# Transposing q and k by DMA instead of on TensorE, in an attention kernel with a gated feed-forward behind it

## The chip, the cores and the metric

The kernel runs on one core of a Trainium2 chip. The metric is the device time of one execution in microseconds (us). The kernel before took 457.21 us, the median of three runs (457.0 to 460.33).

## The reference

There are 8 batches of 8 heads, 576 query positions and a head width of 64. Sixteen "beacon" keys and values stand ahead of the 576 others in every head, so a query sees 592 keys: all beacons, and the keys up to its own position.

```python
k_all = np.concatenate([beacon_k, k], axis=2)          # (8, 8, 592, 64)
v_all = np.concatenate([beacon_v, v], axis=2)
scores = scale * np.matmul(q, k_all.transpose(0, 1, 3, 2))
scores = np.where(causal, -1e9, scores)
a = np.exp(scores - scores.max(-1, keepdims=True))
a /= a.sum(-1, keepdims=True) + 1e-09
x = np.matmul(a, v_all)                                # heads side by side: 4608 tokens x 512
g = x @ w_gate                                         # 512 x 1536
out = (g / (1 + np.exp(-g)) * (x @ w_val)) @ w_out     # 1536 x 512
```

Inputs and the output are fp32. The kernel casts to bf16 and multiplies in bf16.

## The kernel before, in words

**Layout.** q, k and v of one batch are loaded with the position on the partitions: five pieces (`c` = 0 to 4) of up to 128 positions by 8 heads by 64, in fp32 staging tiles `q32`, `k32`, `v32`. VectorE casts q and k to the bf16 tiles `qb` and `kb`, piece by piece; GpSimd casts v to one of two tiles `vb`. The score matmul (line 176) contracts over the head width, so it needs q and k with the head width on the partitions. That is the task of the two transposing functions: for a pair `m` of heads (2 x 64 = 128 columns) they run five TensorE transposes of 128x128 into a PSUM tile `t_ps`, and then one copy brings the whole pair to SBUF, as `qT[m]` or `kT[m]` (128 partitions x 640). There is one PSUM buffer for `t_ps`, the attention outputs `pv_ps` and the transposed `xt_ps` together (pool `att`, one buffer).

**Stages of a batch.** The order of the work is written out by hand, and each engine takes its instructions in that order.

- Attention: for each of the four pairs, `scores1` and `scores2` (matmuls into PSUM, Exp on ScalarE, causal masks on GpSimd), the product with v (`pv`), and `x_transpose`, which writes the result into `xT`. In the gaps stand eight halves of the last feed-forward matmul of the chunk before (`fill`, lines 267 to 278), each second one with a copy to SBUF and a store.
- Feed-forward of 512 tokens: 12 steps `f`, each eight matmuls of 128x512 for the gate and the value (line 244), Silu on ScalarE (254) and a product on VectorE (255). Of the first three steps, three quarters of the matmuls are issued between the last parts of the attention. The big PSUM pool has three buffers, which scores and gate/value products share.
- Preparing the next batch, inside the feed-forward: from step `f_cast` on two casts are issued in each step (lines 364 to 369). When all ten are out, and from step 4 on, one transposing function follows in each step (370); what is left comes behind step 11 (372). k pairs are copied from PSUM by VectorE, q pairs by ScalarE. `f_cast` is 0, but 7 in the first batch, whose data for the next batch are still loading.
- Then SyncE gets the loads of the batch after next (374). They wait until the casts have freed the staging tiles.

The first batch is prepared pair by pair by `prep_first`, in which every step waits for the loads. A last feed-forward of 512 tokens follows the eighth batch. SyncE issues all loads of q, k and v and all stores, in the order of the program; the weights are loaded from GpSimd's queue.

Of the kernel before, what the change touches and what calls it, by code (L numbers as in the profile page):

```python
# [8 lines left out]
ACT = mybir.ActivationFunctionType  # L9
ALU = mybir.AluOpType  # L10
BF16 = mybir.dt.bfloat16
FP32 = mybir.dt.float32

P = 128
# [3 lines left out]
NKT = 5  # L18
KPAD = NKT * P
# [24 lines left out]
def kernel(  # L44
# [12 lines left out]
    nc = tc.nc  # L57
    B, H, Sq, Dq = q.shape
# [7 lines left out]
    NPAIR = H // 2  # L66
    assert NCH == B + 1

    static = ctx.enter_context(tc.tile_pool(name="static", bufs=1))
# [13 lines left out]
    qb = static.tile([P, NKT, H, D], BF16, name="qb")  # L83
    kb = static.tile([P, NKT, H, D], BF16, name="kb")
    vb = [static.tile([P, NKT, H, 68], BF16, name=f"vb{i}") for i in range(2)]
    qT = [static.tile([P, KPAD], BF16, name=f"qT{m}") for m in range(NPAIR)]
    kT = [static.tile([P, KPAD], BF16, name=f"kT{m}") for m in range(NPAIR)]
    pt = [
        (static.tile([P, P1_W], BF16, name=f"p1_{i}"), static.tile([P, P2_W], BF16, name=f"p2_{i}"))
        for i in range(4)  # L90
# [29 lines left out]
    def load_batch(b):  # L120
        load_kv("k32", k, beacon_k, b, 0, H)
        load_q(b, 0, H)
        load_kv("v32", v, beacon_v, b, 0, H)

    def cast_pieces(dst, name, h0, h1, last, engine):
        src = stage[name]

        def main(c0, c1):
            engine.tensor_copy(dst[:, c0:c1, h0:h1, 0:D], src[:, c0:c1, h0:h1, :])  # L129

        def tail():
            engine.tensor_copy(dst[0:last, 4, h0:h1, 0:D], src[0:last, 4, h0:h1, :])

        if h1 - h0 == H:
            return [lambda c=c: main(c, c + 1) for c in range(4)] + [tail]
        return [lambda: main(0, 4), tail]

    def load_w(i):
        cols = slice(384 * i, 384 * i + 384)
        for t, src in ((wg, moe_w_gate), (wv, moe_w_val)):  # L140
            nc.gpsimd.dma_start(t[:, :, cols], src[:, cols].rearrange("(kk p) f -> p kk f", p=P))
# [8 lines left out]
    def transpose_q(m, copy):  # L150
        t_ps = att.tile([P, KPAD], BF16, name="t_ps", tag="att")
        for c in range(NKT):
            nc.tensor.transpose(t_ps[:, P * c : P * c + P], qb[:, c, 2 * m : 2 * m + 2, :], ident[:])  # L153
        copy(qT[m][:, 0:S], t_ps[:, 0:S])

    def transpose_k(m, copy):
        t_ps = att.tile([P, KPAD], BF16, name="t_ps", tag="att")
        for c in range(NKT):
            L = P if c < 4 else 80
            nc.tensor.transpose(  # L160
                t_ps[:, P * c : P * c + L], kb[0:L, c, 2 * m : 2 * m + 2, :], ident[0:L, 0:L]
            )
        copy(kT[m][:, 0 : NB + S], t_ps[:, 0 : NB + S])

    def dve_copy(o, i):
        nc.vector.tensor_copy(o, i)  # L166

    def act_copy(o, i):
        nc.scalar.activation(o, i, ACT.Copy)  # L169

    def scores(m, which, spec, used, masks):
        s = [big.tile([P, 1024], FP32, name="s_ps", tag="big") for _ in range(2)]
# [24 lines left out]
    def scores1(m):  # L197
        scores(m, 0, SCORES1, P1_USED, MASKS1)

    def scores2(m):  # L200
        scores(m, 1, SCORES2, P2_USED, MASKS2)

    def pv(b, m, hh, x):
        h = 2 * m + hh
        o_ps = att.tile([P, NKT, 68], FP32, name="pv_ps", tag="att")
        for c, (q0, _) in enumerate(QBLOCKS):
            for t in range(c + 1):
                w, col = p_slice(t, q0)
                nc.tensor.matmul(  # L209
                    o_ps[:, c, 0 : D + 1],  # L210
                    lhsT=pt[2 * (m % 2) + hh][w][:, col : col + P],
                    rhs=vb[b % 2][:, t, h, 0 : D + 1],
                    start=(t == 0),
                    stop=(t == c),
                )
        rec = rec_pool.tile([P, NKT, 1], FP32, name="rec")
        nc.vector.reciprocal(rec[:], o_ps[:, :, D : D + 1])  # L217
        nc.vector.tensor_tensor(  # L218
            out=x[:, :, D * h : D * h + D],
            in0=o_ps[:, :, 0:D],  # L220
            in1=rec[:].to_broadcast([P, NKT, D]),
            op=ALU.mult,
        )
# [77 lines left out]
    def prep_first(m):  # L301
        h0, h1 = 2 * m, 2 * m + 2
        for f in cast_pieces(kb, "k32", h0, h1, 80, nc.vector):
            f()
        transpose_k(m, dve_copy)
        for f in cast_pieces(qb, "q32", h0, h1, 64, nc.vector):
            f()
        transpose_q(m, dve_copy)
        for f in cast_pieces(vb[0], "v32", h0, h1, 80, nc.gpsimd):
            f()  # L310
# [4 lines left out]
    def fill():  # L315
        if fillers:
            fillers.pop(0)()

    for b in range(B):
        x = x_pool.tile([P, NKT, DM], BF16, name="x")  # L320
        for m in range(NPAIR):
            scores1(m)
            if m:
                pv(b, m - 1, 0, x)
            fill()
            scores2(m)
            if b == 0:
                load_w(m)
                if m + 1 < NPAIR:
                    prep_first(m + 1)  # L330
            if m:
                pv(b, m - 1, 1, x)
            fill()
            if m:
                x_transpose(b, m - 1, x)
        j = b
        last = NPAIR - 1
        gv_mm(j, 0, 0, KD - 1)
        pv(b, last, 0, x)
        gv_mm(j, 1, 0, KD - 1)  # L340
        pv(b, last, 1, x)
        gv_mm(j, 2, 0, KD - 1)
        x_transpose(b, last, x)
        if b == 0:
            load_batch(1)
            for i in range(2):
                load_wo(i)
        casts, trans, vcasts = [], [], []
        if b + 1 < B:
            vcasts = cast_pieces(vb[(b + 1) % 2], "v32", 0, H, 80, nc.gpsimd)  # L350
            casts = cast_pieces(kb, "k32", 0, H, 80, nc.vector) + cast_pieces(
                qb, "q32", 0, H, 64, nc.vector
            )
            for m in range(NPAIR):
                trans.append(lambda m=m: transpose_k(m, dve_copy))
                trans.append(lambda m=m: transpose_q(m, act_copy))
        f_cast = 0 if b else 7
        for f in range(NF):
            if f < 3:
                gv_mm(j, f, KD - 1, KD)  # L360
            else:
                gv_mm(j, f, 0, KD)
            gv_act(j, f)
            if f >= f_cast:
                for _ in range(2):
                    if casts:
                        casts.pop(0)()
                if vcasts:
                    vcasts.pop(0)()
            if not casts and trans and f >= 4:  # L370
                trans.pop(0)()
        while trans:
            trans.pop(0)()
        if b + 2 < B:
            load_batch(b + 2)
        fillers = out_halves(j)
# [39 lines left out]
```

## Time and profile before

| | us |
|---|---|
| median of three runs | 457.21 |
| the profiled execution | 458.49 |
| its span, first to last instruction | 456.8 |
| PE busy | 391.2 (86% of the span) |
| ScalarE busy | 204.0 |
| VectorE busy | 196.8 |
| GpSimd busy | 113.2 |
| TensorE clock granted, mean share of full | 0.988 |
| DMA queue of SyncE, share of 16 engines | 38.1% |

The profile's times are us from the span's start. PE is TensorE's matmuls, PEld its weight loads, DVE is VectorE, ACT is ScalarE, POOL is GpSimd, and SPq is the queue of transfers that SyncE issues: an SPq row is the issuing of a transfer, not its landing. "x5" at the end of a row says that five instructions were merged in it; a bracket behind it gives the idle time before it and what ended that. From the second batch on, one batch takes 47.42 us in the trace.

### The profile page before, as it was taken

The numbers are of one execution on the slowest core, as the hardware profiler recorded it, in microseconds if no ns is written. First come the engines' busy times: TensorE is split into PE (matmuls) and PEld (weight loads), VectorE is DVE, ScalarE is ACT, GpSimd is POOL, SyncE is SP. The second block draws the span as 40 slices with busy tenths as digits, with TensorE's granted clock in tenths as the row PEclk, the third lists the DMA queues.
The fourth block names the chain that finished last, engine by engine and source line by source line (L and its number), as shares of the span: only waits on it lengthen the run. The fifth ranks groups of instructions, "written<-read, shape, count | busy, mean of one in ns | idle before, by whom it ended". The sixth has DMA issues, their size and how long they took to land.

```text
span 456.8 us, 8189 instructions
## 1 busy us (share of the span) xinstructions
PE 391.2 (86%) x3068; PEld 199.8 (44%) x3120; DVE 196.8 (43%) x439; ACT 204.0 (45%) x280; POOL 113.2 (25%) x383
## 2 busy tenths in 40 slices
PE   2357894998988898989898989998998989899995
PEld 1234443454544444544444445444454445444441
DVE  2253452347434552456344634373346434433331
ACT  3324232752476247633763366336743475231120
POOL 3636001460045103430253015400550053000000
PEclk9999997899999999999999999999999999999999
DMA  4999998913921294119510781159110011000011
GB/s 106 173 157 185 193 202 180 217 49 71 214 57 49 67 205 93 48 37 205 102 69 24 171 146 48 47 126 192 47 48 2 0 47 48 0 1 37 33 46 69
DMA packets 127959, 43.53 MB, mean 95 GB/s; under 512 B 117680, under 2 KB 123312, under 8 KB 127920
## 3 DMA queue, kind: packets, MB, share of 16 engines
q1 hardware_dynamic: 122128, 38.29, 38.1%
q0 software_dynamic: 5792, 4.72, 7.0%
q8 instruction: 24, 0.39, 0.4%
q14 instruction: 15, 0.12, 0.1%
HBM read 38.27 MB, written 9.44 MB: 104 GB/s over the span
## 4 chain that ended last, share of the span: by engine, by line
PE 68%; DVE 16%; ACT 6%; SPq 3%; DMA 3%; issue 3%; DVEq 0%; ACTq 0%
PE gv_ps L244 32%; PE o_ps L267 19%; PE pv_ps L209 8%; PE s_ps L176 4%; DVE o_sb L276 4%; DVE hT L255 4%; DMA v<-in_v_dram 3%; DVE xT L231 3%; ACT sg L254 2%; PE t_ps L153 2%; DVE qb L129 2%; ACT L185 2%; PE t_ps L160 1%; DVE kb L129 1%; ACT p L185 1%
## 5 line engine op out<-in xcount | busy, mean ns | idle before, releaser
L187 POOL TENSOR_SCALAR_AFFINE_SELECT p<-p 128x112 bf16<-128x112 bf16 (+2 forms) x320 | 80.3, 285 | 227.3 <-ACT p L185 225.9
L254 ACT ACTIVATE sg<-gv_ps 128x512 bf16<-128x512 f32 x108 | 62.8, 597 | 162.9 <-PE gv_ps L244 155.6
L185 ACT ACTIVATE p<-s_ps 128x720 bf16<-128x720 f32 (+1 forms) x128 | 104.5, 876 | 61.9 <-PE s_ps L176 56.7
L244 PE MATMUL gv_ps<-xT,wg 128*128 128x512 bf16 x414 | 113.8, 380 | 13.1 <-DVE xT L231 7.8
L244 PE MATMUL gv_ps<-xT,wv 128*128 128x512 bf16 x426 | 114.3, 381 | 0.3
L255 DVE TENSOR_TENSOR hT<-sg,gv_ps 128x512 bf16<-128x512 bf16 x108 | 73.6, 685 | 93.1 <-ACT sg L254 93.1
L267 PE MATMUL o_ps<-wo,hT 128*128 128x512 bf16 x404 | 101.0, 384 | 4.3 <-DVE o_sb L276 2.3
L244 PEld LDWEIGHTS <-wv 128*128 128x128 bf16 x432 | 42.3, 98 | 60.1 <-issue 11.2
L267 PEld LDWEIGHTS <-hT 128*128 128x128 bf16 x432 | 38.5, 98 | 46.0 <-issue 8.6
L244 PEld LDWEIGHTS <-wg 128*128 128x128 bf16 x432 | 38.5, 98 | 40.4 <-issue 6.9
L209 PEld LDWEIGHTS <-p 128*128 128x128 bf16 x960 | 37.4, 101 | 24.1 <-issue 9.2
L276 DVE COPY o_sb<-o_ps 128x512 f32<-128x512 f32 x36 | 24.9, 691 | 53.4 <-PE o_ps L267 53.4
L209 PE MATMUL pv_ps<-vb,p 128*128 128x65 bf16 x960 | 42.3, 199 | 6.3 <-DVE xT L231 5.2
L176 PE MATMUL s_ps<-qT,kT 64*128 64x336 bf16 (+5 forms) x384 | 39.5, 307 | 9.3 <-ACT p L185 8.1
L217 DVE RECIPROCAL rec<-pv_ps 128x5 f32<-128x5 f32 x64 | 12.5, 195 | 75.3 <-PE pv_ps L209 75.3
L218 DVE TENSOR_TENSOR x<-pv_ps,rec 128x320 bf16<-128x320 f32 x64 | 31.4, 491 | 2.2
L129 POOL CAST vb<-v 128x512 bf16<-128x512 f32 x32 | 18.5, 612 | 39.8 <-DMA v<-in_v_dram 39.8
L160 PE MATMUL t_ps<-ident,kb 128*128 128x128 bf16 (+1 forms) x160 | 15.0, 231 | 15.0 <-DVE kb L129 12.7
L176 PEld LDWEIGHTS <-kT 64*128 64x128 bf16 x384 | 13.2, 98 | 31.0 <-issue 26.4
L153 PE MATMUL t_ps<-ident,qb 128*128 128x128 bf16 x160 | 15.7, 235 | 10.8 <-DVE kT L166 6.9
L169 ACT ACTIVATE qT<-t_ps 128x576 bf16<-128x576 bf16 x28 | 18.1, 647 | 9.9 <-PE t_ps L153 9.9
L160 PEld LDWEIGHTS <-kb 128*128 128x128 bf16 (+1 forms) x160 | 12.3, 105 | 22.2 <-DVE kb L129 13.7
(28 smaller groups left out, 140.1 us busy)
## 6 DMA issues: line engine op xcount, KB each, us to landing
out_dram<-o_sb SPq DMA_DIRECT2D x36, 256.0 KB, 2.0
q<-in_q_dram SPq DMA_DIRECT2D x71, 128.0 KB, 3.5
k<-in_k_dram SPq DMA_DIRECT2D x64, 96.0 KB, 2.6
v<-in_v_dram SPq DMA_DIRECT2D x64, 96.0 KB, 3.3
k<-in_k_dram SPq DMA_DIRECT2D x7, 224.0 KB, 3.0
v<-in_v_dram SPq DMA_DIRECT2D x7, 224.0 KB, 3.6
wg<-in_moe_w_gate_dram POOLq DMA_DIRECT2D x4, 384.0 KB, 5.5
wv<-in_moe_w_val_dram POOLq DMA_DIRECT2D x4, 384.0 KB, 7.2
```

Source lines behind the costliest of these rows:

```text
L129: engine.tensor_copy(dst[:, c0:c1, h0:h1, 0:D], src[:, c0:c1, h0:h1, :])
L160: nc.tensor.transpose(t_ps[:, P * c : P * c + L], kb[0:L, c, 2 * m : 2 * m + 2, :], ident[0:L, 0:L])
L176: nc.tensor.matmul(s[hh][:, col : col + n], lhsT=kT[m][r, P * t : P * t + P], rhs=qT[m][r, q0 : q0 + n], start=True, stop=True,)
L185: nc.scalar.activation(p[:, 0:used], s[hh][:, 0:used], ACT.Exp, scale=0.125)
L187: nc.gpsimd.affine_select(out=p[:, col : col + n], in_=p[:, col : col + n], compare_op=ALU.is_ge, fill=0.0, base=base, pattern=[[1, n]], c ...
L209: nc.tensor.matmul(o_ps[:, c, 0 : D + 1], lhsT=pt[2 * (m % 2) + hh][w][:, col : col + P], rhs=vb[b % 2][:, t, h, 0 : D + 1], start=(t == 0 ...
L218: nc.vector.tensor_tensor(out=x[:, :, D * h : D * h + D], in0=o_ps[:, :, 0:D], in1=rec[:].to_broadcast([P, NKT, D]), op=ALU.mult,)
L244: nc.tensor.matmul(gv[f][:, TOK * half : TOK * half + TOK], lhsT=w[:, kk, P * f : P * f + P], rhs=xT[:, kk, TOK * j : TOK * j + TOK], star ...
L254: nc.scalar.activation(sg[:], gv[f][:, 0:TOK], ACT.Silu)
L255: nc.vector.tensor_tensor(out=hTs[j][:, f, :], in0=sg[:], in1=gv[f][:, TOK:1024], op=ALU.mult)
L267: nc.tensor.matmul(o_ps[:], lhsT=hTs[j][:, f, P * i : P * i + P], rhs=wo[:, f, :], start=(f == 0), stop=(f == NF - 1),)
L276: nc.vector.tensor_copy(o_sb[:], o_ps[:])
```

## The change

All four `qT` become slices of one tile, and so do the `kT`. A new function transposes one piece `c` of all eight heads by one transfer from SBUF to SBUF: the source is `kb` or `qb`, up to 128 positions by 512 columns, the destination the columns `128 c` and following of all four pairs. SyncE issues it, right behind the cast of that piece in the program. Casts of k and q now alternate, two casts and two transfers in a step. The transposing functions on TensorE remain for the first batch alone (`prep_first`). The built program gives each of the new instructions a block of 16 source rows by 128 columns: 32 blocks for a full piece, 20 for the last piece of k (80 positions) and 16 for the last of q (64).

```diff
-    qT = [static.tile([P, KPAD], BF16, name=f"qT{m}") for m in range(NPAIR)]
-    kT = [static.tile([P, KPAD], BF16, name=f"kT{m}") for m in range(NPAIR)]
+    qT_all = static.tile([P, NPAIR, KPAD], BF16, name="qT")
+    kT_all = static.tile([P, NPAIR, KPAD], BF16, name="kT")
+    qT = [qT_all[:, m, :] for m in range(NPAIR)]
+    kT = [kT_all[:, m, :] for m in range(NPAIR)]
...
+    def dma_transpose(dst, src, c, rows):
+        nc.sync.dma_start_transpose(
+            dst[:, :, P * c : P * c + rows], src[0:rows, c, :, :].rearrange("p h d -> p (h d)")
+        )
+
...
-            casts = cast_pieces(kb, "k32", 0, H, 80, nc.vector) + cast_pieces(
-                qb, "q32", 0, H, 64, nc.vector
-            )
-            for m in range(NPAIR):
-                trans.append(lambda m=m: transpose_k(m, dve_copy))
-                trans.append(lambda m=m: transpose_q(m, act_copy))
+            kc = cast_pieces(kb, "k32", 0, H, 80, nc.vector)
+            qc = cast_pieces(qb, "q32", 0, H, 64, nc.vector)
+            for c in range(NKT):
+                casts.append((kc[c], lambda c=c: dma_transpose(kT_all, kb, c, P if c < 4 else 80)))
+                casts.append((qc[c], lambda c=c: dma_transpose(qT_all, qb, c, P if c < 4 else 64)))
...
                 for _ in range(2):
                     if casts:
-                        casts.pop(0)()
+                        for step in casts.pop(0):
+                            step()
...
-            if not casts and trans and f >= 4:
-                trans.pop(0)()
-        while trans:
-            trans.pop(0)()
+        while casts:
+            for step in casts.pop(0):
+                step()
```

The first place is TensorE at the end of the second batch's feed-forward, where the scores of the third begin. The rows are in the order in which PE takes them; the first fence is the kernel before.

```order
1461 L244 LDWEIGHTS wv
1462 L244 MATMUL gv_ps<-xT,wv 128x512
1463 L153 LDWEIGHTS qb
1464 L153 MATMUL t_ps<-ident,qb 128x128
...
1471 L153 LDWEIGHTS qb
1472 L153 MATMUL t_ps<-ident,qb 128x128
1473 L176 LDWEIGHTS kT_96
1474 L176 MATMUL s_ps<-qT_92,kT_96 128x512
```

The same place in the changed kernel:

```order
1311 L248 LDWEIGHTS wv
1312 L248 MATMUL gv_ps<-xT,wv 128x512
1313 L180 LDWEIGHTS kT
1314 L180 MATMUL s_ps<-qT,kT 128x512
1315 L180 LDWEIGHTS kT
1316 L180 MATMUL s_ps<-qT,kT 128x512
1317 L180 LDWEIGHTS kT
1318 L180 MATMUL s_ps<-qT,kT 128x464
1319 L180 LDWEIGHTS kT
1320 L180 MATMUL s_ps<-qT,kT 128x464
1321 L271 LDWEIGHTS hT
```

The five transposes ahead of the scores are gone, and with them the seven groups of five that stood between the steps before. The scores follow the last feed-forward matmul directly, and the halves of the chunk before (L271) follow the scores.

The second place is SyncE's queue in the feed-forward of the first batch. Before, the loads for the second batch (v last) are followed directly by the loads for the third:

```order
47 L108 DMA v_87<-in_beacon_v_dram 16x8x64
48 L109 DMA v_87<-in_v_dram 112x8x64
49 L113 DMA v_87<-in_v_dram 128x3x64 x8
50 L116 DMA v_87<-in_v_dram 80x8x64
51 L108 DMA k_86<-in_beacon_k_dram 16x8x64
52 L109 DMA k_86<-in_k_dram 112x8x64
```

The same place in the changed kernel:

```order
49 L115 DMA v_87<-in_v_dram 128x3x64 x8
50 L118 DMA v_87<-in_v_dram 80x8x64
51 L168 DMA_TRANSPOSE kT<-kb 128x4x128
52 L168 DMA_TRANSPOSE qT<-qb 128x4x128
...
59 L168 DMA_TRANSPOSE kT<-kb 128x4x80
60 L168 DMA_TRANSPOSE qT<-qb 128x4x64
61 L110 DMA k_86<-in_beacon_k_dram 16x8x64
62 L111 DMA k_86<-in_k_dram 112x8x64
```

Ten transposes now stand in SyncE's queue in every batch but the last: behind every load and store issued so far, and ahead of the 31 loads for the batch after next. The stores of the chunk follow those loads, as before.

## Rows read from the trace of the kernel before

**Rows 1.** The page: the chain that ended last, shares by engine.
```profile
PE 68%; DVE 16%; ACT 6%; SPq 3%; DMA 3%; issue 3%; DVEq 0%; ACTq 0%
```

**Rows 2.** Stretches of the span: attention, then feed-forward, of the third batch.
```profile
core 0: us, PE busy (x) PEld busy (x) DVE busy (x) ACT busy (x) POOL busy (x), PEclk, DMA share, GB/s
127.70:147.40 19.70, 17.61 (x194) 9.21 (x196) 7.25 (x19) 14.84 (x18) 9.73 (x39) 1.00 0.11 42
147.40:175.10 27.70, 25.32 (x174) 13.01 (x177) 15.27 (x33) 9.99 (x18) 3.08 (x7) 1.00 0.70 140
```

**Rows 3.** Timeline of PE, third batch: first full step, transposes, next scores.
```profile
155.61 1.02 PE L244 MATMUL gv_ps<-xT,wg 128*128 128x512 bf16 x4 [0.54 <-DVE hT L255]
173.71 0.44 PE L153 MATMUL t_ps<-ident,qb 128*128 128x128 bf16 x5
174.08 0.59 PE L176 MATMUL s_ps<-qT,kT 64*128 64x512 bf16 x4
177.40 0.47 PE L176 MATMUL s_ps<-qT,kT 64*128 64x80 bf16 x7 [1.19 <-ACT p L185]
```

**Rows 4.** Timeline of PE, first batch: the same steps, nothing between them.
```profile
52.13 1.02 PE L244 MATMUL gv_ps<-xT,wg 128*128 128x512 bf16 x4 [0.55 <-DVE hT L255]
...
67.67 0.42 PE L160 MATMUL t_ps<-ident,kb 128*128 128x128 bf16 x5
...
78.08 1.00 PE L176 MATMUL s_ps<-qT,kT 64*128 64x512 bf16 x4
```

**Rows 5.** Stretches with the granted clock (seventh figure after the bounds, PEclk).
```profile
74.00:76.00 2.00, 0.95 (x8) 0.67 (x7) 0.47 (x1) 0.45 (x1) 0.00 (x0) 0.50 0.51 109
84.00:86.00 2.00, 2.00 (x25) 0.88 (x24) 1.11 (x3) 0.67 (x1) 0.85 (x4) 1.00 1.36 205
```

**Rows 6.** Groups by line: the transposes and copies; busy us, mean ns, idle before.
```profile
L169 ACT ACTIVATE qT<-t_ps 128x576 bf16<-128x576 bf16 x28 | 18.1, 647 | 9.9 <-PE t_ps L153 9.9
L153 PE MATMUL t_ps<-ident,qb 128*128 128x128 bf16 x160 | 15.7, 235 | 10.8 <-DVE kT L166 6.9 <-DVE qb L129 3.9
L166 DVE COPY kT<-t_ps 128x592 bf16<-128x592 bf16 x32 | 14.7, 458 | 7.9 <-PE t_ps L160 7.9
L160 PE MATMUL t_ps<-ident,kb 128*128 128x128 bf16 x128 | 13.6, 235 | 15.0 <-DVE kb L129 12.7 <-ACT qT L169 2.2
```

**Rows 7.** Timeline of ACT, third batch: last copy of q, then the next Exp.
```profile
174.40 0.65 ACT L169 ACTIVATE qT<-t_ps 128x576 bf16<-128x576 bf16 x1
175.07 1.28 ACT L185 ACT_TABLE_LOAD   x1
```

**Rows 8.** Timeline of DVE: casts in the first batch, then in the third.
```profile
62.20 0.75 DVE L129 CAST kb<-k 128x512 bf16<-128x512 f32 x2
...
69.44 0.41 DVE L132 CAST qb<-q 64x512 bf16<-64x512 f32 x1
...
155.47 0.75 DVE L129 CAST kb<-k 128x512 bf16<-128x512 f32 x2
...
160.88 0.41 DVE L132 CAST qb<-q 64x512 bf16<-64x512 f32 x1
```

**Rows 9.** Timeline of SPq: last v load of the first batch; the third's first and last load.
```profile
68.47 0.43 SPq L116 DMA_DIRECT2D v<-in_v_dram  x1
...
155.92 0.34 SPq L108 DMA_DIRECT2D k<-in_beacon_k_dram  x1
...
173.00 0.43 SPq L116 DMA_DIRECT2D v<-in_v_dram  x1
```

**Rows 10.** Line L101 from 162 to 167.6: issue ns min/median/max, then landing.
```profile
L101 SPq DMA_DIRECT2D q<-in_q_dram x8: 372/500/508, 162.3 to 166.4; - x8
...
DMA to landing us min/median/max: 3.2/3.4/3.6
```

**Rows 11.** Line L101 from 59 to 61: the last q loads for the second batch.
```profile
L101 SPq DMA_DIRECT2D q<-in_q_dram x2: 1911/2110/2310, 56.8 to 59.2; - x2
...
DMA to landing us min/median/max: 5.6/6.6/7.6
```

**Rows 12.** Line L278 from 179 to 240: the stores, issue ns min/median/max, then landing.
```profile
L278 SPq DMA_DIRECT2D out_dram<-o_sb x7: 332/357/363, 180.0 to 237.4; - x7
...
DMA to landing us min/median/max: 2.0/2.0/2.4
```

**Rows 13.** DMA queues: packets, MB, share of 16 engines' span.
```profile
q1 hardware_dynamic: 122128, 38.29, 38.1%
```

More of the change, by code (lines that the diff above doesn't have):

```diff
@@ L163, in transpose_k @@
         copy(kT[m][:, 0 : NB + S], t_ps[:, 0 : NB + S])
+    def dma_transpose(dst, src, c, rows):
+        nc.sync.dma_start_transpose(
+            dst[:, :, P * c : P * c + rows], src[0:rows, c, :, :].rearrange("p h d -> p (h d)")
+        )
     def dve_copy(o, i):
         nc.vector.tensor_copy(o, i)
-    def act_copy(o, i):
-        nc.scalar.activation(o, i, ACT.Copy)
     def scores(m, which, spec, used, masks):
@@ L347 @@
                 load_wo(i)
-        casts, trans, vcasts = [], [], []
+        casts, vcasts = [], []
         if b + 1 < B:
             vcasts = cast_pieces(vb[(b + 1) % 2], "v32", 0, H, 80, nc.gpsimd)
-            casts = cast_pieces(kb, "k32", 0, H, 80, nc.vector) + cast_pieces(
-                qb, "q32", 0, H, 64, nc.vector
-            )
-            for m in range(NPAIR):
-                trans.append(lambda m=m: transpose_k(m, dve_copy))
-                trans.append(lambda m=m: transpose_q(m, act_copy))
+            kc = cast_pieces(kb, "k32", 0, H, 80, nc.vector)
[3 more added lines that the diff above has]
+                casts.append((qc[c], lambda c=c: dma_transpose(qT_all, qb, c, P if c < 4 else 64)))
         f_cast = 0 if b else 7
```

## The prediction, as it was put on record

> **What bounds the kernel now.** I first asked which engine carries the chain that ended last: PE, with 68% of it [rows 1]. Then I looked at the stages of a later batch, since a share of the whole span says nothing of one stage. In both PE is the busiest: 17.61 of 19.70 us in the attention, 25.32 of 27.70 in the feed-forward, where ACT has 9.99 and DVE 15.27 [rows 2]. So an instruction taken off PE in the feed-forward shortens the batch, if nothing else is late there. The timeline of PE gives the amount [rows 3, 4], and the queue of SyncE [rows 9] shows when the transfers that replace it could start.
>
> **What is removed.** The groups by line price the transposes as 160 + 128 matmuls (and 32 smaller ones) of 235 ns [rows 6], but they are pipelined, so I do not multiply. The same nine steps of the feed-forward (f = 3 to 11) stand in the trace with and without transposes between them. In the third batch they and the eight groups take 174.08 - 155.61 = 18.47 us [rows 3]; in the first batch, whose transposes come later, 67.67 - 52.13 = 15.54 us [rows 4]. The difference, 2.93 us, is what the 40 transposes and their waits cost PE in a batch. Batches 2 to 7 prepare a successor in this way: 6 x 2.93 = **17.6 us**.
>
> Does it reach the end? After the scores PE waits 1.19 us for the first Exp [rows 3]. ACT reaches its table load at 175.07, directly after the q copy that ends at 175.05 [rows 7]. The copy goes too, and the Silu before it and the scores come 2.93 us earlier, so ACT moves with PE. The 28 copies of 647 ns on ACT and 28 of the 32 of 458 ns on DVE [rows 6] otherwise lie beside PE's work: 0.
>
> **What is added.** Ten transfers in a batch: eight of 32 blocks, one of 20, one of 16. Let T be the time from one full transfer to the next. The last is issued 8.6 T after the first (eight full ones and 20/32). No row shows T. Its bounds:
>
> - Nearest row, by what is read: a q load reads 512 pieces of 256 bytes, and so does a full transfer (128 rows x 4 groups of 128 bf16). q loads follow one another every 0.50 us and land 3.4 us after issue [rows 10]. A store, half of whose 256 KB would be a transfer's bytes, takes 0.36 us and lands after 2.0 [rows 12]; I take 0.33, its least, as the lower end.
> - Upper end, by what is written: a block of 16 rows leaves 16 neighbours of 2 bytes, 32 bytes, on each of 128 partitions, 4,096 pieces in a full transfer. The mean packet of SyncE's queue costs 38.1% x 16 x 456.8 us / 122,128 = 22.8 ns of one engine [rows 13], so 4,096 on 16 engines are 5.8 us.
>
> I take T = **1.0 us**, near the q load: once its price for reading, once more for the finer writing. For the landing I take 3.4 us.
>
> A rule bears on this. The Trainium skill, "Advanced Engine Details and Errata", section X-Bar Transpose (TRN2), says that transposing DMAs are as fast as regular ones, at about 90% of a copy's bandwidth; by that T would be some 0.55 us (an estimate), and the sum below about 438. No row here shows a transposing transfer.
>
> **Steady batches.** The first cast of k ends near 155.9 [rows 8], where SyncE also stood ready for the loads [rows 9]. The last transfer lands at 155.9 + 8.6 T + 3.4, with T = 1.0 at 167.9. The last cast ends at 161.3 [rows 8], earlier than the last issue, so it does not bind. The scores would start at 155.61 + 15.54 = 171.15, and their second pair of matmuls, which needs the last piece of q, 0.4 us later: 171.6. Cover: 3.7 us, gone at T = (171.6 - 159.3) / 8.6 = **1.43 us**. Beyond that each batch waits on PE, and the halves of the chunk before, which could fill the time, stand behind the waiting scores in PE's order. Cost at T = 1.0: 0.
>
> **First batch.** Here the transfers stand behind the loads for the second batch in SyncE's queue, and the last of these is issued at 68.47 + 0.43 = 68.90 [rows 9]. The last transfer lands at 68.9 + 8.6 + 3.4 = 80.9. Before, the scores started at 78.08 [rows 4], their second pair 0.4 later. Cost: 80.9 - 78.5 = **+2.4 us**. PE had a thin stretch here anyway: the granted clock was 0.50 (1.2 of 2.4 GHz) from 74 on, and 1.00 again by 84, some 6 us after the scores began [rows 5]. In the changed kernel PE is idle from 67.67 on, so I expect the same dip, later by the same 2.4 us, at no further cost.
>
> A second wait is added here. Casts of k and q alternate, so the first q cast comes second instead of sixth, at 62.6, and the last q loads of 128 positions land at 64.4 and 64.8 [rows 8, 11]. DVE stands 2.2 us, with eight casts and the products of steps 8 to 11 queued behind. Even if it made up nothing, its last cast would end at 72.1 instead of 69.85 [rows 8]; SyncE gets to it at 77.5. PE, which could wait for a product in its last step, idles until 80.9 after that. Cost: 0.
>
> **Queues moved past.** The 31 loads occupied SyncE from 155.92 to 173.43 [rows 9]; behind ten transfers (9.1 us) they end near 183. They are used by the casts of the next batch, some 44 us after 155.9, so about 14 us of cover remain. The chunk's stores come after the loads: the first at 183 instead of 180.0, landing by 185.4 [rows 12]. The copies alternate between three buffers, so the fourth waits for it. The seventh store was issued at 237.4, a batch earlier 190.0: two steps of 5 us from the first, which puts the fourth copy near 195, now 192. Cover 6.6 us, gone at T = 1.7: it costs 0.
>
> **Sum.** The profiled execution took 458.49 us (span 456.8 and 1.7 around it), 1.28 above the median of the runs. 458.49 - 17.6 + 2.4 = 443.3; less 1.28: **442 us** as a median.
>
> As a function of T, beyond 1.43: change = -17.6 + 6 x (8.6 T - 12.3) + (8.6 T - 6.2) = 60.2 T - 97.6. It is zero at T = 1.62.
>
> **Rivals.**
>
> 1. *The transfers are slow; the kernel becomes slower.* The place is PE's wait at the head of each batch, the price 60.2 us for each us of T beyond 1.62. At T = 2 it is 480 us, at 2.7 it is 522; at the upper end, 5.8, it is +252: 709 us. For it: 4,096 pieces of 32 bytes, ten transfers with only 15.7 us from first cast to use, and no row of such a transfer. Against it: the queue moves 512 pieces of 256 bytes in 0.50 us. Chance 0.28: 0.12 for T up to 2.66, 0.06 up to 4 and 0.10 beyond, where the pieces are priced one by one.
> The Trainium skill, "VectorE: DVE Perf Modes", section The three transpose paths, gives 1,309 ns for a 128x128 transpose by DMA against 390 ns on TensorE, and advises TensorE where PSUM will do. A batch has 292 blocks, 36.5 such squares, 47.8 us if they follow one another: T = 5.2, an estimate near 675 us. No run here shows whether squares overlap.
> 2. *The gain is given back.* T between 1.54 and 1.70: the batches wait as long as the transposes took, and the time stays within 1% (452.6 to 461.8). Chance 0.06; the stretch is narrow.
> 3. *The first boundary gains too.* With T at 0.33 and the landing of a store, the last transfer follows the last cast (72.1 + 2.0 = 74.1, 4.4 us before 78.5). 458.49 - 17.6 - 4.4 - 1.28 = 435 us. Chance 0.10. At T = 0.50 it is 437.7.
>
> That the transposes stay on PE somewhere is excluded by the order of the instructions: PE issues 40 only, in the first preparation.
>
> **How the numbers follow.** The forecast (T from about 0.5 to 1.54, 438 to 452) has 0.56, the fast rival 0.10, the same 0.06, the slow one 0.28. About 1% is what a measurement of this kernel can tell from no change. Faster by over 1%: 0.66; within: 0.06; slower: 0.28. The range starts at 434 (rival 3) and must reach into the slow rival until no more than 0.2 is left out: I stop at T = 2.66, 520 us, with some 0.16 beyond. The forecast's own range is 437 to 452.
>
> **What would show it.** PE's timeline: the scores of batches 3 to 8 start 15.5 us after the first full step, without a wait for a transfer; a wait there is rival 1 or 2, and its length is 8.6 T - 12.3. SyncE's queue: the spacing of the transposes is T. The first batch: the scores start near 81, with the half clock until about 87. The batch's period: 44.5 us instead of 47.42. ACT's table load comes right behind the last Silu or the scores. I am wrong if T exceeds 1.4, if the transposes slow other transfers so that a cast waits for a load, or if PE's steps stretch while they run.

## The result and the profile after

The changed kernel took **445.34 us** (median of 4 runs, 445.02 to 445.98), the kernel before, run beside it, 458.26 (4 runs, 457.0 to 460.33). The ratio is 0.9715, interval 0.9671 to 0.976: some 2.8% faster. The forecast was 442 in a range of 434 to 520. The profiled execution took 445.03 us (span 443.3), that of the kernel before 458.49 (456.8): 13.46 us less.

The page of the changed kernel, its DMA queue that answers to [rows 13] and its chain that answers to [rows 1]:

```profile
q1 hardware_dynamic: 157072, 46.67, 46.8%
...
PE 70%; DVE 10%; DMA 6%; SPq 6%; issue 4%; ACT 3%; DVEq 0%; ACTq 0%
```

PE still carries the end. SPq, SyncE's queue, has doubled its share of the chain, and its packets have grown by 34,944, 499 for each of 70 transfers.

ACT's timeline in the changed kernel (start us, us, operation; in brackets the idle time before it and what ended it) has one table load per batch ahead of the Exp; it answers to [rows 7] and measures the period:

```profile
83.84 1.28 ACT L189 ACT_TABLE_LOAD   x1 [15.16 <-PE s_ps L180]
...
129.65 1.28 ACT L189 ACT_TABLE_LOAD   x1
...
174.39 1.28 ACT L189 ACT_TABLE_LOAD   x1 [0.44 <-PE s_ps L180]
...
218.70 1.28 ACT L189 ACT_TABLE_LOAD   x1
...
263.02 1.28 ACT L189 ACT_TABLE_LOAD   x1
```

From 174.39 on the loads are 44.31 and 44.32 us apart; before they were 47.42 apart from the third batch on (the second, which began at the half clock, took 48.50). So a later batch gains **3.10 us**. Batches 2 to 7 are the six that were freed of the transposes. Five gain this much; the one from 129.65 to 174.39 takes 44.74 us and gains 2.68, because PE waits there for a transfer (0.32 at 173.95, below). Together that is **18.2 us**. The loads at 218.70 and 263.02 have no bracket: ACT goes on without waiting. The rest of the account is the first boundary. PE's timeline in the changed kernel, answering to [rows 3, 4]:

```profile
67.02 1.03 PE L248 MATMUL gv_ps<-xT,wv 128*128 128x512 bf16 x4
...
80.88 0.61 PE L180 MATMUL s_ps<-qT,kT 64*128 64x512 bf16 x2 [12.84 <-DMA qT<-qb]
...
83.22 0.57 PE L180 MATMUL s_ps<-qT,kT 64*128 64x464 bf16 x2 [1.73 <-DMA qT<-qb]
...
88.59 0.59 PE L180 MATMUL s_ps<-qT,kT 64*128 64x512 bf16 x4
...
105.97 0.38 PE L248 MATMUL gv_ps<-xT,wg 128*128 128x512 bf16 x1 [1.33 <-DVE xT L235]
...
113.30 1.02 PE L248 MATMUL gv_ps<-xT,wg 128*128 128x512 bf16 x4 [0.55 <-DVE hT L259]
...
173.95 0.37 PE L180 MATMUL s_ps<-qT,kT 64*128 64x464 bf16 x2 [0.32 <-DMA qT<-qb]
...
202.35 1.02 PE L248 MATMUL gv_ps<-xT,wg 128*128 128x512 bf16 x4 [0.55 <-DVE hT L259]
...
217.98 0.59 PE L180 MATMUL s_ps<-qT,kT 64*128 64x512 bf16 x4
...
221.03 0.47 PE L180 MATMUL s_ps<-qT,kT 64*128 64x80 bf16 x7 [0.92 <-ACT p L189]
```

The same view of the kernel before, with the later steps of its first boundary:

```profile
84.36 0.59 PE L176 MATMUL s_ps<-qT,kT 64*128 64x512 bf16 x4
...
100.87 0.38 PE L244 MATMUL gv_ps<-xT,wg 128*128 128x512 bf16 x1 [0.45 <-DVE xT L231]
...
108.20 1.02 PE L244 MATMUL gv_ps<-xT,wg 128*128 128x512 bf16 x4 [0.54 <-DVE hT L255]
```

Read down the two columns of starts: the second scores stand at 88.59 against 84.36 (4.2 us late), the first full step at 113.30 against 108.20 (5.1 late). Between the two lies a wait that was 0.45 and is 1.33. So the boundary lost 4.2 us to late transfers and 0.9 to something else. At the other end 0.4 us is gained behind PE's last matmul: from the issue of the last store to the end of the span it is 3.0 us (440.34 to 443.3), before it was 3.4 (453.43 to 456.8). The whole difference is -18.2 + 5.1 - 0.4 = -13.5. In the later batches the scores start 217.98 - 202.35 = 15.63 us after the first full step, where [rows 3] had 18.47.

SyncE's queue, answering to [rows 9], and the line of the transfers (issue ns min/median/max, then landing):

```profile
68.94 1.32 SPq L168 DMA_TRANSPOSE kT<-kb  x1
...
80.82 1.20 SPq L168 DMA_TRANSPOSE qT<-qb  x1
...
100.64 2.53 SPq L282 DMA_DIRECT2D out_dram<-o_sb  x3
...
157.96 1.28 SPq L168 DMA_TRANSPOSE kT<-kb  x1
...
169.80 1.20 SPq L168 DMA_TRANSPOSE qT<-qb  x1
...
189.93 5.04 SPq L282 DMA_DIRECT2D out_dram<-o_sb  x4
```

```profile
L168 SPq DMA_TRANSPOSE kT<-kb x35: 1202/1217/1923, 68.9 to 346.9; - x35
L168 SPq DMA_TRANSPOSE qT<-qb x35: 1197/1206/1560, 70.4 to 348.2; - x35
...
DMA to landing us min/median/max: 2.3/2.4/4.6
```

From the first to the last of ten transfers there are nine spacings: (169.80 - 157.96) / 9 = 1.32 us, and 11.88 / 9 = 1.32 at the first boundary. **T is 1.32 us**, the landing 2.4. The small transfers (20 and 16 blocks), the last two of a batch, were priced at 0.6 and 0.5 of a full one; the one of 169.80 has 16 blocks and took 1.20 us to issue, like the others.

DVE's timeline in the changed kernel, answering to [rows 8]:

```profile
65.08 0.43 DVE L131 CAST qb<-q 128x512 bf16<-128x512 f32 x1 [2.42 <-DMA v<-in_beacon_v_dram]
...
70.30 0.41 DVE L134 CAST qb<-q 64x512 bf16<-64x512 f32 x1
...
104.87 0.69 DVE L280 COPY o_sb<-o_ps 128x512 f32<-128x512 f32 x1 [1.46 <-DMA out_dram<-o_sb]
```

The first line is the wait that the change added (the releaser named is the transfer that landed last; the q cast needs a q load). The last is the place of the 0.9 us: a copy waits for a store that was issued at 100.64, behind the transfers and the loads, and PE's step at 105.97 waits for the xT copy that stands behind it on DVE. The run with five output buffers below tests this.

Stretches with the granted clock (seventh figure after the bounds), answering to [rows 5]:

```profile
core 0: us, PE busy (x) PEld busy (x) DVE busy (x) ACT busy (x) POOL busy (x), PEclk, DMA share, GB/s
...
72.00:74.00 2.00, 0.00 (x0) 0.00 (x0) 0.00 (x0) 0.00 (x0) 1.18 (x3) 0.50 0.44 89
...
86.00:88.00 2.00, 2.00 (x14) 0.77 (x13) 0.00 (x0) 1.72 (x4) 1.04 (x4) 0.68 0.97 216
88.00:90.00 2.00, 1.85 (x24) 0.88 (x23) 0.89 (x2) 1.45 (x3) 1.46 (x6) 1.00 0.39 83
```

PE did nothing from 72 to 74 and was granted half of full speed (1.2 of 2.4 GHz); full speed came back during 86 to 88. The ten transfers leave the DMA engines room: the share in 72 to 74 is 0.44, less than in 86 to 88 where the loads run.

### The profile page after: what moved, and what is told of

Same layout as the page of the kernel before. It is cut to its first block, busy times and chain, and to the rows that moved or that the text cites. A ratio compares the mean times of both kernels' runs of the same rounds, so it can differ in the third digit from the quotient of the medians.

```text
span 443.3 us, 7678 instructions
## 1 busy us (share of the span) xinstructions
PE 373.3 (84%) x2791; PEld 183.3 (41%) x2840; DVE 186.1 (42%) x411; ACT 187.8 (42%) x252; POOL 113.4 (26%) x383
## 4 chain that ended last, share of the span: by engine, by line
PE 70%; DVE 10%; DMA 6%; SPq 6%; issue 4%; ACT 3%; DVEq 0%; ACTq 0%
PE gv_ps L248 38%; PE o_ps L271 19%; PE pv_ps L213 8%; PE s_ps L180 4%; DVE o_sb L280 4%; DVE xT L235 3%; DMA v<-in_v_dram 3%; SPq L168 2%; ACT sg L258 2%; DVE hT L259 2%; DMA qT<-qb 1%; ACT p L189 1%; PE xt_ps L232 1%; DMA out_dram<-o_sb 1%; SPq L106 1%
## 5 line engine op out<-in xcount | busy, mean ns | idle before, releaser
L271 PE MATMUL o_ps<-wo,hT 128*128 128x512 bf16 x401 | 99.6, 383 | 4.5 <-DVE o_sb L280 2.3
L248 PEld LDWEIGHTS <-wg 128*128 128x128 bf16 x432 | 40.8, 98 | 50.5 <-issue 7.4
L180 PE MATMUL s_ps<-qT,kT 64*128 64x336 bf16 (+5 forms) x384 | 39.9, 306 | 22.7 <-DMA qT<-qb 14.9
L271 PEld LDWEIGHTS <-hT 128*128 128x128 bf16 x432 | 38.4, 98 | 45.0 <-issue 7.3
L180 PEld LDWEIGHTS <-kT 64*128 64x128 bf16 x384 | 13.5, 98 | 47.2 <-issue 40.2
L131 DVE CAST kb<-k 128x512 bf16<-128x512 f32 x32 | 13.7, 429 | 11.3 <-DMA k<-in_k_dram 11.2
L235 DVE COPY xT<-xt_ps 128x576 bf16<-128x576 bf16 x32 | 14.4, 451 | 8.9 <-PE xt_ps L232 8.9
L232 PE MATMUL xt_ps<-ident,x 128*128 128x128 bf16 (+2 forms) x160 | 14.2, 221 | 2.4 <-DVE x L222 2.4
```

Source lines behind the costliest of these rows:

```text
L180: nc.tensor.matmul(s[hh][:, col : col + n], lhsT=kT[m][r, P * t : P * t + P], rhs=qT[m][r, q0 : q0 + n], start=True, stop=True,)
L235: nc.vector.tensor_copy(xT[:, m, S * b : S * b + S], t_ps[:])
L248: nc.tensor.matmul(gv[f][:, TOK * half : TOK * half + TOK], lhsT=w[:, kk, P * f : P * f + P], rhs=xT[:, kk, TOK * j : TOK * j + TOK], star ...
L271: nc.tensor.matmul(o_ps[:], lhsT=hTs[j][:, f, P * i : P * i + P], rhs=wo[:, f, :], start=(f == 0), stop=(f == NF - 1),)
```

## The experiments

The theory: PE was freed of the transposes in six batches, the transfers are hidden there, and what is lost at the first boundary is SyncE's price for each transfer. Every time is a median, with its ratio to the kernel before run on the same chip. Line numbers are those of each kernel.

**No transfers at all** (e_none): what do they cost?

```diff
-    casts.append((kc[c], lambda c=c: dma_transpose(kT_all, kb, c, P if c < 4 else 80)))
-    casts.append((qc[c], lambda c=c: dma_transpose(qT_all, qb, c, P if c < 4 else 64)))
+    casts.append((kc[c],))
+    casts.append((qc[c],))
```

> Left out: q and k of batches 2 to 8 are cast but not transposed at all, so every batch scores the first batch's q and k. Theory A (the gain is TensorE's transposes, 3.1 us in each of six steady batches, and the transfers are hidden there; the one loss is the first boundary, where ten transfers of 1.31 us stand behind the loads): the steady batch stays at 44.3 us, as in the changed kernel, and the first scores of batch 2 start near 68 instead of 83, without the dip of the clock (some 1.4 us): 458.5 - 18.6 - 10.1 - 1.4 = about 428 us. Rival B (the transfers also slow the steady batches, by sharing SBUF and the DMA engines with matmuls and loads): the steady batch falls below 44.3 us, and the time below 425.

Measured: 433.54 us, 0.9463 (0.9436 to 0.949). ACT's timeline of e_none:

```profile
162.10 1.28 ACT L189 ACT_TABLE_LOAD   x1
...
206.41 1.28 ACT L189 ACT_TABLE_LOAD   x1
```

The table loads stand at 117.78, 162.10, 206.41 and 250.73, so the later batches take 44.31 to 44.32 us, as with transfers: in these the transfers are hidden. The second batch however took 48.45 from its table load (69.33) to the next, 4.1 more, which no theory had. PE's timeline of this kernel shows the place:

```profile
92.45 0.38 PE L248 MATMUL gv_ps<-xT,wg 128*128 128x512 bf16 x1 [2.19 <-DVE xT L235]
```

With the scores from 67.77 on the output copies come earlier, and the fourth waits 2.3 us for a store. PE was busy 0.26 us of the stretch 90 to 92, and the granted clock fell afterwards:

```profile
90.00:92.00 2.00, 0.26 (x2) 0.00 (x0) 0.66 (x2) 0.56 (x1) 2.00 (x5) 1.00 0.75 287
...
94.00:96.00 2.00, 2.00 (x7) 0.67 (x5) 0.69 (x2) 0.00 (x0) 0.00 (x0) 0.50 0.00 0
```

So early scores meet another limit at this boundary, the three output buffers.

**TensorE for the second batch, transfers for the others** (e_hybrid).

```diff
-    for c in range(NKT):
-        casts.append((kc[c], lambda c=c: dma_transpose(kT_all, kb, c, P if c < 4 else 80)))
...
+    if b == 0:
+        casts = [(p,) for p in kc + qc]
+        for m in range(NPAIR):
+            trans.append(lambda m=m: transpose_k(m, dve_copy))
+            trans.append(lambda m=m: transpose_q(m, act_copy))
+    else:
+        for c in range(NKT):
+            casts.append((kc[c], lambda c=c: dma_transpose(kT_all, kb, c, P if c < 4 else 80)))
...
```

> The second batch's q and k are transposed on TensorE as in the kernel before; only batches 3 to 8 use the transfers. Theory A: the first boundary returns to 78.1 us for the scores and gives back the 5.1 us (4.7 of the queue, 0.9 of the stores behind the late loads, less rounding), while the six steady batches keep 3.1 us each: about 440 us. Rival C (the loss of 5.1 us came from the changed order of the casts, which made VectorE wait for a q load, or from the one tile for all pairs): nothing or little is given back, 444 to 445 us.

Measured: 441.09 us, 0.9644 (0.9594 to 0.9694), some 4 us below the changed kernel. The two intervals overlap a little, so the trace has to decide: PE's first full step of the second batch stands at 106.99, where the changed kernel has 113.30 and the kernel before 108.20. The first boundary is where the changed kernel loses. Of these 6.3 us some 2 are given back, since PE waited 1.59 and 1.46 us behind an output copy in two later batches. This version also puts the casts of the second batch back into their old order; e_none, which keeps the new order and has its scores from 67.77 on, shows that the order is not what made them late.

**Each transfer twice** (e_double): the first one into a tile that nobody reads.

```diff
-    casts.append((kc[c], lambda c=c: dma_transpose(kT_all, kb, c, P if c < 4 else 80)))
+    kr, qr = (P, P) if c < 4 else (80, 64)
+    casts.append((kc[c], lambda c=c, r=kr: dma_transpose(kT_2, kb, c, r),
+                  lambda c=c, r=kr: dma_transpose(kT_all, kb, c, r)))
...
```

> Every transfer is issued twice, first into a tile that nobody reads, then as in the changed kernel: 20 transposing transfers a batch. Theory A (SyncE's issue of 1.31 us for each is the limit, and beyond the cover each batch waits on TensorE): the last one of a steady batch lands 19 x 1.31 + 2.4 us after the first issue, near 185.3 instead of 173.6 in the third batch: 11.6 us in six batches and 13.1 us at the first boundary, about 445 + 83 = 528 us. Rival E (the transfers have spare room, in that two to the same engines overlap, or most of the 1.31 us is waiting for a cast): under 490 us.

Measured: 539.69 us, 1.1787 (1.1758 to 1.1817). The list of waits of this kernel (us in total, times, longest):

```profile
PE s_ps L182 <- DMA qT<-qb: 99.4, 14, 22.7
```

PE now waits for transfers before every batch but the first, two waits each (14 times): this is what rival 1 of the prediction describes. With T doubled to 2.64 its formula gives 60.2 x 2.64 - 97.6 = +61; it was +82. Part of the gap is the formula's 8.6 T, 22.7 us here, where 19 spacings of 1.32 are 25.1. The expectation counts them, and the measured landing, and is 12 us too low. It has no term for the clock, whose mean over the span fell to 0.892 (0.980 in the changed kernel); no run shows how much of the 12 us that is.

**The transposes put back on PE without their copies** (f_pe; their results are not used, the transfers remain), and the same with all casts of k ahead of those of q, as before (g_pe): is it PE's own time or the waits?

```diff
+            if b:
+                for m in range(NPAIR):
+                    trans.append(lambda m=m: transpose_k(m, no_copy))
+                    trans.append(lambda m=m: transpose_q(m, no_copy))
...
+            if not casts and trans and f >= 4:
+                trans.pop(0)()
```

> The changed kernel, with the 240 TensorE transposes of the six steady batches put back at their old places, into PSUM that nobody reads: no copies to SBUF. Theory A (what the change saves in a steady batch is mostly TensorE's own time): eight groups at 0.26 to 0.28 us each are 2.2 us a batch, 13 us in all, 458 us, of 3.1 us the rest being waits for the copies. Rival B (the saving is the copies of VectorE and ScalarE and the one PSUM buffer that they hold): 445 to 447 us.

Measured: 469.31 us, 1.0237 (1.0214 to 1.026), 11 us more than theory A expected. PE's timeline of f_pe:

```profile
166.52 0.23 PE L162 MATMUL t_ps<-ident,kb 128*128 128x128 bf16 x1 [0.36 <-DVE kb L131]
...
167.78 0.21 PE L162 MATMUL t_ps<-ident,kb 80*128 80x80 bf16 x1 [1.04 <-DVE kb L134]
```

The transposes now wait for casts of k that alternate with casts of q, 1.4 us a batch. That is a wait of this experiment, not of the kernel before, so the experiment was run again with the order mended:

> As the version with TensorE's transposes put back and no copies, but with the five casts of k ahead of those of q, as in the kernel before, so that no transpose waits for a cast. Theory A (of the 3.1 us that a steady batch gained, 2.2 to 2.5 are TensorE's own time for 40 transposes; the version tried lost 1.4 us more in each batch to the alternating casts): 46.5 to 46.8 us a batch, 458 to 460 us. Rival B (the copies and their PSUM buffer were the gain): 44.3 us a batch, 445 us. Rival I (putting transposes between the steps costs 3.8 us whatever the casts do): 468 us.

Measured: 458.3 us (10 runs), 1.0006 (0.999 to 1.0022). PE's timeline of g_pe:

```profile
161.65 1.02 PE L251 MATMUL gv_ps<-xT,wg 128*128 128x512 bf16 x4 [0.54 <-DVE hT L262]
...
179.54 0.58 PE L183 MATMUL s_ps<-qT,kT 64*128 64x512 bf16 x4
```

No bracket is left on a transpose, and the stretch takes 17.89 us against 15.63 with transfers alone. The period is 46.51 (table loads at 133.69, 180.20, 226.72): 2.2 of the 3.1 us a batch are PE's own time for 40 transposes, and the 0.9 up to 47.42 are waits, for copies within the stretch (18.47 - 17.89 = 0.6) and for the first Exp after it (1.19 before, 0.87 here).

**One transfer for each pair of heads** (e_pair): casts write qb and kb pair by pair, eight transfers of 40 blocks follow the last cast, and the first scores need only the first pair.

```diff
-    qb = static.tile([P, NKT, H, D], BF16, name="qb")
-    kb = static.tile([P, NKT, H, D], BF16, name="kb")
+    qb = static.tile([P, NPAIR, NKT, P], BF16, name="qb")
+    kb = static.tile([P, NPAIR, NKT, P], BF16, name="kb")
...
+    casts = [(p,) for p in kc + qc]
+    for m in range(0, NPAIR, 1):
+        casts[-1] += (
+            lambda m=m: dma_transpose(kT_all, kb, m, m + 1),
+            lambda m=m: dma_transpose(qT_all, qb, m, m + 1),
+        )
```

> q and k are cast into tiles whose columns are ordered pair by pair, and one transfer takes all five pieces of one pair (40 blocks, 8 transfers a batch instead of 10, all behind the last cast); the scores of a pair wait for that pair alone. Theory A, with a price of 1.3 us for each transfer whatever its size between 16 and 40 blocks: at the first boundary the second transfer is issued near 71.3 and lands near 74, so the scores start 9 us earlier than in the changed kernel and the stores no longer wait: about 435 us; SyncE's spacing stays 1.3 us. Rival D (the price goes with the blocks, 1.31 us for 32): spacing 1.6 us, scores near 74.5, about 436 us; the spacing tells the two apart, not the time. Rival C (the loss is not the queue's): 444 us or more.

Measured: 451.91 us, 0.9872 (0.9827 to 0.9916): a miss of 17 us. Up to the scores all went as expected: they stand at 74.55, without a second wait. PE's timeline of e_pair, later, and its list of waits:

```profile
104.90 0.58 PE L268 MATMUL gv_ps<-xT,wg 128*128 128x512 bf16 x1 [7.70 <-DVE xT L255]
```

```profile
DVE o_sb L300 <- DMA out_dram<-o_sb: 14.8, 5, 7.8
```

The stores were issued from 100.44 on, after transfers and loads as in the changed kernel. PE reached its step at 97.2 (in the changed kernel at 104.6), and waited 7.70 us; DVE has four more such waits later. So the theory of the first boundary was incomplete: two things come late there, the transposed tiles and the stores.

**Five output buffers instead of three**, in the changed kernel (f_o5), in e_pair (f_pair_o5) and, as a control, in the kernel before (g_before_o5).

```diff
-    o_pool = ctx.enter_context(tc.tile_pool(name="o", bufs=3))
+    o_pool = ctx.enter_context(tc.tile_pool(name="o", bufs=5))
```

> The changed kernel with five output buffers instead of three. Theory A (of the 5.1 us lost at the first boundary, 0.9 is the fourth copy of an output block, which waits for a store that stands behind the late loads): the wait of 1.3 us on TensorE at 104 falls to 0.45, the sixth-batch rhythm stays 44.3 us, 444.4 us. Rival G (the wait there is for something else that is late in the same way, such as the products with v): no change of that wait, 445.3 us.

> One transfer for each pair, as tried before, with five output buffers. Theory A (that version lost its earlier scores to the fourth copy, which waited 7.8 us for a store behind transfers and loads in SyncE's queue): the waits for stores go, the scores of batch 2 start near 74.6, every later batch takes 44.3 us, and 9.1 us of the first boundary are gained on the changed kernel: 436 us. Rival H (the transfers behind the last cast make each batch late in another way): 444 us or more.

> The kernel before with five output buffers instead of three: a control. Theory A (the waits for stores came with the transfers in SyncE's queue; before, the stores of the first chunk were issued from 87.6 on): no change, 457 to 459 us. Rival J (the output buffers were short already): 455 or less.

Measured: f_o5 took 444.74 us, 0.9706 (0.9676 to 0.9736). Its list of waits has none for a store, and PE's wait at the step in question is 0.45 us (at 105.76), as in the kernel before: so the 0.9 us was the wait for an output buffer. The stretch from the Silu table load to the next Exp table load is 0.88 us shorter (104.33 and 129.44, 25.11 apart, against 103.66 and 129.65); in the time of the whole kernel that is too little to tell. f_pair_o5 took 436.74 us, 0.9522 (0.9495 to 0.9549): 15 us from the same edit. g_before_o5 took 458.4 us, 1.0006 (0.9989 to 1.0022): no change. In these runs the buffers are worth much only where the scores come early.

**What sets T: the transfer or its blocks?** Two pairs in one transfer (g_two_o5: 80 blocks, four transfers) and all four (f_one_o5: 160 blocks, two transfers), both on f_pair_o5.

```diff
-    for m in range(0, NPAIR, 1):
+    for m in range(0, NPAIR, 2):
...
-        lambda m=m: dma_transpose(kT_all, kb, m, m + 1),
+        lambda m=m: dma_transpose(kT_all, kb, m, m + 2),
```

> One transfer of 160 blocks for all of k and one for all of q, behind the last cast, with five output buffers. Theory A with a fixed price of SyncE for a transfer (1.2 to 1.3 us, whatever its blocks): SyncE is free 2.6 us after the last cast; the transfers themselves read 2,560 pieces of 256 bytes each, 3.7 us at 22.8 ns on 16 engines, so q lands some 10 us after the last cast: scores of batch 2 near 80, steady batches 44.3 us or up to 1 us more, about 441 us. Rival D (the price goes with the blocks, 1.31 us for 32): each is issued for 6.5 us, the scores of batch 2 start near 85 and each steady batch waits some 4 us: about 470 us.

> One transfer for two pairs (80 blocks, four a batch), five output buffers. SyncE's price of a transfer was 1.2 us for 16 to 40 blocks and 3.1 us for 160. If the price is the larger of 1.2 us and 20 ns a block: 1.6 us each, the second issued near 71.8 and landing some 3.3 us later: scores of batch 2 near 75.2, 437 us. If it is a base and an amount for each block (0.6 us and 16 ns): 1.9 us each, scores near 75.6, 438 us. The spacing in SyncE's queue tells them apart.

Measured: f_one_o5 439.82 us, 0.9596 (0.9575 to 0.9616); g_two_o5 436.35 us, 0.9514 (0.9484 to 0.9545), with the scores at 75.36. The line of the transfers in f_one_o5, then in g_two_o5:

```profile
L187 SPq DMA_TRANSPOSE kT<-kb x7: 2987/3119/3664, 70.2 to 333.7; - x7
...
DMA to landing us min/median/max: 4.9/5.0/6.1
```

```profile
L187 SPq DMA_TRANSPOSE kT<-kb x14: 1371/1438/1839, 69.7 to 334.0; - x14
...
DMA to landing us min/median/max: 3.4/3.5/4.1
```

160 blocks take neither the price of one transfer (1.2 us) nor five times that of 32 blocks, but 3.1 us. 80 blocks take 1.44 and a spacing of about 1.55, where the two forms left after f_one_o5 said 1.6 (the larger of 1.2 us and some 20 ns a block) and 1.9 (a base plus a price per block). The larger-of form comes nearer; two sizes above 40 blocks are few for a rule. What makes the 20 ns is not shown. The DMA share (the last figure but one) points to the DMA engines rather than to SyncE. In f_one_o5 it was

```profile
72.00:76.00 4.00, 0.00 (x0) 0.00 (x0) 0.00 (x0) 0.00 (x0) 2.13 (x4) 0.50 1.08 200
```

and in g_two_o5 1.13 from 71.5 to 76, while in the changed kernel it was 0.51 from 72 to 80, with the engines idle between one transfer and the next. This fits a pace set by SyncE's issue up to 40 blocks (in f_pair_o5 the share was 0.65 and 0.62 from 74 to 78) and by full engines from 80 on; no run changed the one without the other.

**Both repairs and the second batch's first pair on PE** (g_best): f_pair_o5, where in the second batch PE's two groups transpose the first pair, while the other three pairs are transferred.

```diff
-    for m in range(0, NPAIR, 1):
+    if b == 0:
+        casts[-1] += (lambda: transpose_k(0, dve_copy), lambda: transpose_q(0, act_copy))
+    for m in range(0 if b else 1, NPAIR):
```

> One transfer for each pair and five output buffers; for the second batch alone, the first pair is transposed on TensorE (ten matmuls, two copies), which idles there, and pairs 2 to 4 come by transfer. Theory A (what is left at the first boundary is the time from the last cast, near 70, to the landing of the first two transfers): k of the first pair is on TensorE at 70.3, its copy ends near 70.8, q's copy near 72.0, so the scores start near 72 instead of 74.6, and the shorter gap spares part of the half clock: 432 to 434 us, against 436.7. Rival K (the second pair's transfers then come too late, or the clock falls all the same): 435 to 437 us.

Measured: **431.66 us** (431.02 to 434.22), 0.9434 (0.9398 to 0.947), a little under the expected 432 to 434 and below both kernels. PE's timeline of g_best, and two stretches with the clock:

```profile
72.01 0.59 PE L203 MATMUL s_ps<-qT,kT 64*128 64x512 bf16 x4 [0.74 <-ACT qT L196]
```

```profile
68.00:70.00 2.00, 0.23 (x5) 0.13 (x3) 1.63 (x4) 0.60 (x1) 0.51 (x1) 1.00 0.92 201
70.00:72.00 2.00, 0.44 (x5) 0.35 (x5) 0.78 (x2) 0.65 (x1) 1.99 (x4) 1.00 0.34 69
```

The scores start 9 to 11 us earlier than in the changed kernel, the granted clock stays at 1.00 from 66 to 76, and the period is 44.31 as in the changed kernel.

## Why the prediction was right, and where its sizes were off

**Removed: 2.93 us a batch predicted, 3.10 measured.** The mechanism is shown by g_pe: 2.2 us are PE's, 0.9 waits. The same steps gained 18.47 - 15.63 = 2.84 us; the rest is the wait for the first Exp, 0.92 at 221.03 instead of the 1.19 of [rows 3], which the prediction saw but did not price. Six batches gave 18.2 instead of 17.6, since one of them lost 0.4 to a late landing.

**Added: T was taken as 1.0 and is 1.32.** The bounds of 0.33 and 5.8 held, but they are far apart, and that 1.0 came so near was luck: the doubling for the finer writing was a choice and no row's. The row was also misread: 0.50 is the time that a q load's issue takes, and the loads of [rows 10] follow one another every (166.4 - 162.3) / 7 = 0.59 us. The form was wrong too: the last transfer is issued nine spacings after the first, not 8.6, because the price does not follow the blocks (up to 40, as the runs with other sizes show).

A full transfer follows the last after 1.32 us, a q load that reads as much after 0.59 [rows 10], while the DMA engines had room (a share of 0.51 from 72 to 80); four 128x128 squares take 0.33 us each of that spacing. The Trainium skill, "Advanced Engine Details and Errata", section X-Bar Transpose (TRN2), has transposing DMAs as fast as regular ones; the spacing in this trace does not agree. Where the transfers fill the engines it comes near: f_one_o5 moved 200 GB/s from 72 to 76, the loads of the changed kernel 216 from 86 to 88. The Trainium skill, "VectorE: DVE Perf Modes", section The three transpose paths, has 1,309 ns for one square; here a transfer of four squares followed the last after 1.32 us, so the estimate of 675 us, for which squares follow one another singly, fell.

**Steady batches: cost 0 predicted; 0 in five of six, 0.4 in one.** The periods of e_none show it: 44.31 or 44.32 throughout, where the changed kernel has 44.74 once. With nine spacings and a landing of 2.4 the cover is less than the 3.7 us predicted: in the fourth batch the last transfer is issued at 214.47 and lands near 216.9, and the second pair of scores is due 0.4 after 217.98, so 1.5 us are left. A batch earlier one landing of 4.1 us used it up and PE waited 0.32 (the line at 173.95). In the prediction's own numbers, with nine spacings and 2.4, the cover is gone at (171.6 - 155.9 - 2.4) / 9 = 1.48 us, not 1.43; the measured T is only 0.16 below.

**First batch: +2.4 predicted, +4.2 measured. This is the step that failed in size.** 68.9 + 11.9 + 2.4 = 83.2 is where the second pair of scores stands, 4.7 after 78.5; half a microsecond of that was made up by the second scores. The longer T costs 3.3 us of it, and a landing shorter than the 3.4 assumed gives 1.0 back. The clock dip came as said, with full speed back in 86 to 88 (about 87 was said).

**The added DVE wait: 2.2 predicted, 2.42 measured, at no cost here.** The last cast ended at 70.7, and SyncE came to it at 80.8. The late transfers hide it: in e_none, where the scores come early, PE waits 0.71 us for a product of DVE at that place.

**Queues moved past: 0 predicted; 0 in the steady batches, 0.9 us at the first boundary.** This step failed too: it was worked out for steady batches alone. There the first store moved from 180.0 to 189.9, and no copy waited. At the first boundary, where the loads run late and SyncE is behind from the start, the fourth copy's wait took 0.9. It was small only because the late scores hid it: as soon as they came early, in e_pair, it was 7.7.

**The sum.** On the profiled execution 443.3 was said. With 0.6 less for the steady batches, 1.8 more for the late scores, 0.9 for the store and 0.4 less behind the last matmul it is 445.0; measured 445.03. So the errors partly cancel. The median, 445.34, lies 3.3 above the forecast, inside its own range of 437 to 452.

**The rivals.** Rival 1 fell, but its mechanism is real: with doubled transfers the kernel is 82 us slower than before. By the formula it begins at a T of 1.62, 0.3 above the measured one. Rival 2 needed T from 1.54 on, rival 3 a T of 0.33. The slow side's 0.28 rested in part on 4,096 pieces written by a full transfer. The queue's packets say otherwise: a batch has 4,992 more than before here, 5,376 in e_pair and 5,184 in f_one_o5, which fits 16 for each block and 32 for each transfer, 544 for a full one. No run showed a price for each written piece.

## What to carry to other kernels

When transposes move from a busy engine to a DMA queue, count spacings between transfers on that queue and add the landing; the gain is whole where the first cast leads the use by more than that, and beyond it each batch waits (with doubled transfers it was a large loss; no run lies between). Work out the first boundary by itself, since there the queue is already behind. And list what stands behind the new transfers in the same queue: loads had cover here, stores with three buffers hardly any, and that cover shrinks when something else gets faster.

## What the runs showed of the hardware

- The issue of a transposing transfer on SyncE took, as a median, 1.20 to 1.27 us for 16 to 40 blocks of 16x128, 1.44 for 80 and 3.1 for 160. The median landing after issue was 2.4 us in the changed kernel, 2.6 for 40 blocks, 3.5 for 80, 5.0 for 160. At 160 blocks the DMA share was 1.08 and 200 GB/s were moved, in the changed kernel the share was 0.51 from 72 to 80.
- 40 transposes between matmuls cost PE 2.2 us a batch (g_pe), 55 ns each, where their records show 219 ns each.
- After PE's wait of 2.19 us in e_none the granted clock was 0.50 in 94 to 96 although PE was busy all of that stretch. In g_best PE was busy 0.23 us of 68 to 70 and 0.44 of 70 to 72, and the clock stayed at 1.00.
